# A fused attention and mixer kernel: words of U, V and the first weights moved to other steps, the first low-rank rows split by VectorE, V's second copy made by one transfer, the first product's beginning reordered

## The chip, the cores and the metric

The kernel runs on one core of one Trainium2 chip. The metric is the device time of one execution in microseconds (us). Before the change three runs gave 650.47, 652.05 and 653.36 us, a median of 652.05 us. A core has a TensorE for matrix products (PE in the profile; its weight loads are PEld), a VectorE (DVE), a ScalarE (ACT), a GpSimd (POOL), and a SyncE (SP) that here only issues DMA transfers. Each engine works through its own list of instructions in order and waits for others by semaphores. Matrix products write PSUM; everything else lies in SBUF or in DRAM.

## The reference

The first half is attention with a decaying state. For each of 4 batches and 8 heads the sequence of 768 is cut into blocks of 64. A block's output is its masked scores times v, plus its scaled queries times a state that every block passes on:

```python
    for b in range(nb):
        intra = np.einsum('bhic,bhjc->bhij', qb, kb) * Dmask[None]
        intra = np.einsum('bhij,bhjd->bhid', intra, vb)
        inter = np.einsum('bhid,bhde->bhie', qb * lam_pow[None], kv_state)
        out[:, :, sl] = intra + inter
        kv_state = lam_block[None, :, None, None] * kv_state + np.einsum('bhsd,bhse->bhde', kb_dec, vb)
```

The heads are put side by side to x of shape (4, 768, 512). The second half mixes x along the sequence through a product of rank 32 and adds a two-layer network:

```python
    xt = x.transpose(0, 2, 1)
    h = xt @ U @ V
    u = x + h.transpose(0, 2, 1)
    ch = np.maximum(u @ w_ch1, 0.0) @ w_ch2
    return (u + ch).astype(np.float32)
```

U is 768x32, V 32x768, w_ch1 512x2048, w_ch2 2048x512. These four arrive as float64 and are turned into float32 on the chip: the kernel reads them as pairs of 32-bit words.

## The kernel before

**Steps of the front.** The attention half is a list of 24 steps, one for each tile of 128 rows of the sequence: steps 0 to 5 are batch 0, 6 to 11 batch 1, and so on. The list `pieces` is written out by hand, and every engine gets its instructions in that order; no scheduler changes it. A step s holds, among others: the transposes of the next tile's q and k on TensorE (L361) and their copies by ScalarE (qt, kt, L367), the products of weights with v (px, L459), the state's product (pkv, L431) and its sum by VectorE (kv, L437, L439, L442), the products with the state (L470), the copy of the result to x by ScalarE (x_nat, L476), the next scores (pss, L408) and their masking by VectorE (sm, L417). GpSimd scales q (qs, L392) and k (ks, L381). Each step loads 256 KB each of q, k and v some steps ahead (L282): q and k are issued by SP, v by ScalarE's queue.

**The mixer inside the front.** At the end of a batch (s = 5, 11, 17) `low` multiplies the batch's x by U (pp, L486) and ScalarE copies that to p_f (L495). `low_rows` then makes two steps: `own`, which cuts each of four groups of 32 rows into a high part (ScalarE, L532) and a low part (GpSimd, L533) within the tile `vp`, and `other`, four transfers on SP that copy them to the neighbouring group (L543). From step 7 on `mix` (L566) multiplies V's rows by them, and x is corrected (L578), transposed (L629), split (L643, L644, L636) and stored (L594). TensorE reaches the first `mix` after step 7's products.

**Words turned to weights, aside.** U, V and the first two column blocks of w_ch1 are converted in small pieces that hang on steps: `side` maps a step's number to pieces, and `aside(s)` issues them at a place of step s. Each conversion has the pieces: the load of words (SP, L146), *one* (VectorE, L166 and L155, and two ScalarE activations, L173 and L174), *two* (L184), *three* (L192), *four* (L197). What a piece gives to ScalarE is put off to the place `late` of the same or the next step. V then is cut: VectorE makes the high part (`five`, L719), ScalarE copies it to two groups of rows of `vp` (four copies, L726), and VectorE and GpSimd make the low part for one group each (L730). A column block of w_ch1 has three more: *five* (ScalarE, L215), *six* (VectorE, L220), *seven* (VectorE, L227).

**The first product.** After step 23 the PSUM pools change and `hidden` runs units: two groups of 512 rows (a pair) against one block of w_ch1, 16 products to pz (L838), 8 to pd (L849), then ScalarE and VectorE join them (L845, L854) and SP stores r. The first units use the four groups that are ready; in between, as the list `rest` says by unit and place, the last batch is finished: its `low` (L486), its rows, the products pu (L573) and their sums (x_nat, L574), the transposes `turn` (put, L607) with their split (L612, L613, L616). The last pieces of the second block of w_ch1 follow units 0 and 1. There are 48 units in all, then 96 steps of the second product (L970, L972, L974); from unit 4 on the change touches nothing.

Of the kernel before, what the change touches and what calls it, by code (L numbers as in the profile page):

```python
# [8 lines left out]
FP32 = mybir.dt.float32  # L9
F32R = mybir.dt.float32r  # L10
U32 = mybir.dt.uint32
# [7 lines left out]
def kernel(  # L19
# [84 lines left out]
    def tmp(name):  # L104
        return wconv.tile([P, C], FP32, tag="tmp", bufs=2, name=name)
# [391 lines left out]
    def low_rows(b):  # L497

        pp = pps.pop(b)
        own = [(slice(g * R, (g + 1) * R), slice(g * P, (g + 1) * P)) for g in range(G)]  # L500
        if b == B - 1:
            t = tmp("p_h")[0:R]
            h, h2, l, l2 = (p_hl[g * R : (g + 1) * R] for g in range(G))
            for rows, cols in own:
                nc.vector.tensor_scalar(
                    t[:, cols].bitcast(U32), pp[rows].bitcast(U32), HI, None, ALU.bitwise_and
                )

            def low_part():
                for rows, cols in own:  # L510
                    nc.vector.tensor_tensor(
                        out=l[:, cols], in0=pp[rows], in1=t[:, cols], op=ALU.subtract
                    )

            def spread():
                nc.scalar.copy(h, t)
                nc.scalar.copy(h2, t)

            def spread_low():
                nc.scalar.copy(l2, l.bitcast(FP32))  # L520

            pps[b] = [spread, low_part, spread_low]
            return


        def place(g, of, low):
            return p_hl[g * R : (g + 1) * R, low * 2 * P + (of % 2) * P :][:, 0:P]

        def own():
            for g in range(G):  # L530
                rows, at = pp[g * R : (g + 1) * R], place(g, g, 0)
                nc.scalar.copy(at, rows)  # L532
                nc.gpsimd.tensor_tensor(  # L533
                    out=place(g, g, 1), in0=rows, in1=at.bitcast(FP32), op=ALU.subtract
                )

        def other():
            for g in range(G):
                at, of = (
                    p_hl[x * R : (x + 1) * R].rearrange("r (l h c) -> r l h c", l=2, h=2)  # L540
                    for x in (g ^ 1, g)
                )
                nc.sync.dma_start(  # L543
                    out=at[:, :, g % 2].bitcast(FP32), in_=of[:, :, g % 2].bitcast(FP32)
                )

        pps[b] = [own, other]
# [105 lines left out]
    for s in range(NS):  # L653
# [8 lines left out]
        step += [("split", done - 1)] * turns  # L662
        step += [("next_of_low", b - 1)] * (s == NT)
        step += [("prep", s + 1)] * more
# [16 lines left out]
        step += [("masked", s + 1)] * more  # L681
        step += [("low_rows", b)] * (more and c == NT - 1)
        step += [("aside", s)] * (s in (0, NT - 2, NT - 1, NT))
        step += [("store", done)] * (done >= 0 and done // TG < FG)
# [17 lines left out]
    def v_steps():  # L702
# [7 lines left out]

        def parts(gs):
            for half in range(2):
                rows, cols = slice(half * R, (half + 1) * R), slice(half * SH, (half + 1) * SH)
                for g in gs:
                    yield v_hl[g * R : (g + 1) * R, cols], rows

# [7 lines left out]
        def high():  # L724
            for out, rows in parts((0, 2)):
                nc.scalar.copy(out, st["t"][rows])  # L726

        def low(g, engine):
            for out, rows in parts((g,)):
                engine.tensor_tensor(  # L730
                    out=out, in0=st["v"][rows], in1=st["t"][rows], op=ALU.subtract
                )

        halves = [moe_V[:, half * SH : (half + 1) * SH] for half in range(2)]
        return weight_steps(dst, halves, SH, 2 * R, in_parts=True) + [
            five, lambda: low(1, nc.vector), lambda: low(3, nc.gpsimd),
        ]

# [5 lines left out]
    for steps, at in (  # L744
        (u_side, (-1, 1, 1, 2, 2)),
        (v_steps(), (0, 0, 3, 3, 4, 4, 4, 5, 5)),
        (w1_steps(0, True, True), (8, 9, 10, 11, 12, 14, 15, 16, 17, 17, 20, 21)),
        (w1_steps(1, True, True), (14, 15, 16, 17, 18, 22, 23, NS, NS, NS, NS, NS)),
    ):
        assert len(steps) == len(at)  # L750
        for step, n in zip(steps, at):
            side.setdefault(n, []).append(step)
# [24 lines left out]
    for name in "vkvq":  # L777
        load_next(name)
    aside(-1)
    load_next("k")  # L780
# [13 lines left out]
    on_scalar_late(NS)  # L794
    last = side.pop(NS)
    assert not side
    front_ctx.close()
# [87 lines left out]
    def run_units(units, side, every=lambda i: None):  # L885
# [11 lines left out]
        (0, 14, "next_of_low", b), (0, 14, "next_of_low", b), (0, 14, "next_of_low", b),  # L897
        (0, 18, "turn", c0 - 1), (0, 22, "mix", c0),
    ]
# [7 lines left out]
    head = [(pair, ft) for two in (pairs[:2], pairs[2:]) for ft in (0, 1) for pair in two]  # L907
    side = list(zip((0, 0, 0, 0, 1), last)) + list(zip((0, 3, 3, 3, 4, 4, 4, 4), w1_steps(2)))
    for i, (pair, ft) in enumerate(head):
# [164 lines left out]
```

## Time and profile before

| what | value |
|---|---|
| runs shown | 650.47, 652.05, 653.36 us; median 652.05 us |
| the profiled execution's own time | 651.64 us |
| its span, first to last instruction | 649.8 us |
| PE busy | 639.3 us (98% of the span) |
| DVE, ACT, POOL busy | 435.9, 268.1, 116.6 us |
| granted TensorE clock | 1.000 |
| transfers | 131.69 MB, mean 203 GB/s |
| span of the front (steps 0 to 23) | 0 to 114.8 us |
| units 0 and 1 of the first product | 114.8 to 131.6 us |

The profile is of one execution. Its times start at the first instruction. A view of waits puts the idle time of an engine down to what ended it; "issue" is time in which an engine waited for nothing that the profile shows. A timeline's line gives start, duration, engine, line of the kernel, operation and tiles. A view by windows gives the busy time of each engine in a stretch and, at its end, the granted clock, the mean share of the 16 DMA engines and the GB/s that they moved; that share adds up the times of packets and passes 1 where they overlap.

### The profile page before, as it was taken

The page shows a single profiled execution, that of the slowest core. Times are in us where ns is not written, and L with a number is a line of the kernel's source. Part 1 is how long each engine was busy: PE and PEld are TensorE (multiplying, and loading weights), DVE is VectorE, ACT ScalarE, POOL GpSimd, SP SyncE. Part 2 cuts the span into 40 slices and gives each one's busy share as a digit, 9 for nine tenths or more (in the row PEclk, how much of TensorE's full clock was granted, in tenths as well). Part 3 has the DMA queues.
Part 4 walks back from the last instruction along what each step waited for, and adds up shares of the span by engine and source line. Part 5 has one row for each costly group of instructions (what it writes and reads, how often), then busy time and mean ns, then how long its engine had stood idle before and what let it go on. Part 6 is the DMA issues. An engine that isn't in the chain of part 4 may idle for free.

```text
span 649.8 us, 13407 instructions
## 1 busy us (share of the span) xinstructions
PE 639.3 (98%) x5242; PEld 538.5 (83%) x5242; DVE 435.9 (67%) x713; ACT 268.1 (41%) x497; POOL 116.6 (18%) x104
## 2 busy tenths in 40 slices
PE   9999989999999999999999999999999999999997
PEld 8889989788888888888888888888888888888886
DVE  6666868668997777777796244675575665755854
ACT  4675756435664444444455221332322322322320
POOL 4475968240000000000000000030030300300300
PEclk9999999999999999999999999999999999999999
DMA  9989985264776655565587999864363363453521
GB/s 227 249 208 250 249 218 159 84 209 169 287 274 210 211 210 211 210 211 211 210 291 261 325 333 381 301 209 149 97 226 98 114 210 98 161 163 98 178 82 65
DMA packets 132737, 131.69 MB, mean 203 GB/s; under 512 B 81538, under 2 KB 90754, under 8 KB 132674
## 3 DMA queue, kind: packets, MB, share of 16 engines
q1 hardware_dynamic: 107552, 124.41, 58.9%
q10 hardware_dynamic: 25122, 6.42, 4.4%
q8 instruction: 41, 0.67, 0.4%
q14 instruction: 22, 0.18, 0.1%
HBM read 80.09 MB, written 50.33 MB: 201 GB/s over the span
## 4 chain that ended last, share of the span: by engine, by line
PE 94%; ACT 2%; DMA 1%; DVE 1%; issue 1%; ACTq 0%; DVEq 0%
PE pz L838 26%; PE pz L972 13%; PE pz L970 13%; PE pd L974 13%; PE pd L849 13%; PE px L459 4%; PE pss L408 3%; PE px L470 2%; PE pqk L361 2%; PE pkv L431 1%; PE pm L566 1%; DMA qraw<-in_q_dram 1%; PE pp L486 1%; DMA kraw<-in_k_dram 1%; PE pm L629 1%
## 5 line engine op out<-in xcount | busy, mean ns | idle before, releaser
L838 PE MATMUL pz<-u_hl,w 128*128 128x512 f32 x768 | 184.4, 390 | 0.0
L838 PEld LDWEIGHTS pz<-u_hl,w 128*128 128x128 f32 x768 | 143.6, 188 | 30.1 <-ACT r L845 0.3
L972 PE MATMUL pz<-w_hl,m 128*128 128x512 f32 x384 | 148.6, 389 | 0.0
L970 PE MATMUL pz<-w_hl,m 128*128 128x512 f32 x384 | 148.3, 389 | 0.0
L974 PE MATMUL pd<-w_d,m 128*128 128x512 f32 x384 | 147.3, 389 | 0.0
L953 ACT ACTIVATE m<-rm 128x512 fp32r<-128x512 f32 x96 | 60.6, 632 | 182.4 <-PE pd L974 130.4
L954 DVE SCALAR_TENSOR_TENSOR m<-rm,m 128x512 fp32r<-128x512 f32 x96 | 71.5, 747 | 95.8 <-ACT m L953 95.8
L999 POOL TENSOR_TENSOR o<-o,u 128x512 f32<-128x512 f32 x20 | 29.8, 1521 | 433.0 <-DVE o L995 433.0
L854 DVE SCALAR_TENSOR_TENSOR r<-pd,r 128x512 f32<-128x512 f32 x96 | 61.7, 684 | 60.5 <-ACT r L845 48.2
L849 PE MATMUL pd<-u_d,w 128*128 128x512 f32 x384 | 95.9, 390 | 0.0
L970 PEld LDWEIGHTS pz<-w_hl,m 128*128 128x128 f32 x384 | 72.1, 188 | 15.1
L972 PEld LDWEIGHTS pz<-w_hl,m 128*128 128x128 f32 x384 | 72.1, 188 | 14.9
L974 PEld LDWEIGHTS pd<-w_d,m 128*128 128x128 f32 x384 | 72.1, 188 | 14.9
L849 PEld LDWEIGHTS pd<-u_d,w 128*128 128x128 f32 x384 | 71.8, 188 | 14.8
L845 ACT ACTIVATE r<-pz 128x512 f32<-128x512 f32 x96 | 51.7, 590 | 65.0 <-PE pz L838 65.0
L955 DVE SCALAR_TENSOR_TENSOR m<-m 128x512 fp32r<-128x512 f32 x96 | 74.7, 779 | 3.0
L417 DVE TENSOR_TENSOR sm<-pss,mask 128x512 f32<-128x512 f32 x48 | 30.9, 684 | 18.6 <-PE pss L408 18.6
L215 ACT ACTIVATE w<-wf 128x512 fp32r<-128x512 f32 x32 | 20.3, 633 | 38.6 <-DVE wf L197 30.7
L173 ACT ACTIVATE sc<-sc,ends 128x512 f32<-128x512 uint32 x30 | 21.6, 720 | 22.8 <-DVE sc L166 22.8
L459 PE MATMUL px<-vraw,sm 128*64 128x64 f32 x768 | 28.3, 225 | 1.0 <-issue 0.7
L408 PE MATMUL pss<-qt,kt 64*128 64x128 f32 x384 | 28.6, 289 | 0.4 <-ACT kt L367 0.4
L392 POOL TENSOR_TENSOR qs<-qt,powq 128x512 f32<-128x512 f32 x20 | 26.0, 1300 | 15.3 <-ACT qt L367 15.1
(92 smaller groups left out, 606.5 us busy)
## 6 DMA issues: line engine op xcount, KB each, us to landing
r_d<-r SPq DMA_DIRECT2D x96, 256.0 KB, 2.5
rm<-r_d SPq DMA_DIRECT2D x96, 256.0 KB, 2.7
words<-in_moe_w_ch_dram SPq DMA_DIRECT2D x30, 512.0 KB, 4.3
w_d<-w SPq DMA_DIRECT2D x16, 768.0 KB, 3.4
w_hl<-w_d SPq DMA_DIRECT2D x16, 512.0 KB, 6.0
u_d<-x_nat SPq DMA_DIRECT2D x24, 256.0 KB, 4.1
u<-u_d SPq DMA_DIRECT2D x24, 256.0 KB, 4.3
qraw<-in_q_dram SPq DMA_DIRECT2D x23, 256.0 KB, 4.8
```

The lines of the kernel that those rows point to most:

```text
L408: nc.tensor.matmul(out=pss[:, x, a, :], lhsT=kt[half[x], a, :], rhs=qt[half[x], a, :], start=True, stop=True,)
L459: nc.tensor.matmul(out=px[half[t], x, a, :], lhsT=sm[:, x, a, half[t]], rhs=vr[:, 2 * a + x, :], start=(a == 0), stop=(alone and a == HP - 1),
L838: nc.tensor.matmul(out=like(acc[g][0], g), lhsT=w[:, n, ct, :], rhs=columns(uhl[g][:, n], g, ct), start=(ct == 0 and n == 0), stop=(ct == ...
L845: nc.scalar.mul(rs[g], acc[g][0], 4096.0 + 1.0)
L849: nc.tensor.matmul(out=like(acc[g][1], g), lhsT=w[:, 2, ct, :], rhs=columns(ud[g], g, ct), start=(ct == 0), stop=(ct == CT - 1),)
L854: nc.vector.scalar_tensor_tensor(rs[g], acc[g][1], 4096.0, rs[g], ALU.mult, ALU.add)
L953: nc.scalar.activation(out=m[:, 0], in_=r, func=AF.Relu, scale=NEAR)
L954: nc.vector.scalar_tensor_tensor(m[:, 1], r, 0.0, hi, ALU.max, ALU.subtract)
L955: nc.vector.scalar_tensor_tensor(m[:, 2], hi, E, low, ALU.mult, ALU.subtract)
L970: nc.tensor.matmul(out=pz, lhsT=m[:, 0, cols], rhs=hl[:, 0], start=first, stop=False)
L972: nc.tensor.matmul(out=pz, lhsT=m[:, 1, cols], rhs=hl[:, 1], start=False, stop=end)
L974: nc.tensor.matmul(out=pd, lhsT=m[:, 2, cols], rhs=dd, start=first, stop=end)
```

## The change

1. U's words are loaded in step 1 and not ahead of step 0; *one* and *two* run in step 3, *three* and *four* in step 4.
2. V's words are loaded in step 2; *one* and *two* in step 4, *three*, *four*, `five` and `low` in step 5. ScalarE copies the high part to one group (two copies), VectorE makes one low part, and one SP transfer (`again`, 64 partitions of 768 elements) copies both to the other two groups; GpSimd has no part in it.
3. The first batch's `own` runs in step 5. VectorE cuts off the high part from p_f (one 128x128 instruction) and copies it to the four groups; GpSimd's four subtractions read it. ScalarE does none of it. For batches 1 and 2 `own` is as before.
4. The words of w_ch1's block 0 are loaded in steps 6, 7, 9, 11 (before 8 to 11), those of block 1 in steps 18 to 21 (before 14 to 17), its *one* in step 22 (before 18).
5. *three* to *six* of block 1 run ahead of the first product's unit 0, not behind it; *seven* behind unit 0, not unit 1.
6. The last batch's rows: ScalarE copies the four high parts straight from PSUM, VectorE subtracts, ScalarE makes the second copies. The second `turn` of unit 0 stands at place 15, not 18.

On the engines' lists the order of TensorE's instructions changes in that one `turn` alone. VectorE's list of step 5 and 6 reads: sm of step 6, the cut of p_f, four copies, V's *three*, *four*, `five`, two of `low`, kv of step 7, sm of step 7.

```diff
         def own():
+            high = tmp("p_h")[:, 0:P] if b == 0 else None
+            if b == 0:
+                nc.vector.tensor_scalar(
+                    high.bitcast(U32), pp.bitcast(U32), HI, None, ALU.bitwise_and
+                )
             for g in range(G):
                 rows, at = pp[g * R : (g + 1) * R], place(g, g, 0)
-                nc.scalar.copy(at, rows)
-                nc.gpsimd.tensor_tensor(
-                    out=place(g, g, 1), in0=rows, in1=at.bitcast(FP32), op=ALU.subtract
-                )
+                if b == 0:
+                    nc.vector.tensor_copy(out=at, in_=high[g * R : (g + 1) * R])
+                    top = high[g * R : (g + 1) * R]
+                else:
+                    nc.scalar.copy(at, rows)
+                    top = at.bitcast(FP32)
+                nc.gpsimd.tensor_tensor(out=place(g, g, 1), in0=rows, in1=top, op=ALU.subtract)
...
-        step += [("next_of_low", b - 1)] * (s == NT)
...
+        step += [("next_of_low", b)] * (s == NT - 1)
...
         def high():
-            for out, rows in parts((0, 2)):
+            for out, rows in parts(0):
                 nc.scalar.copy(out, st["t"][rows])
-        def low(g, engine):
-            for out, rows in parts((g,)):
-                engine.tensor_tensor(
+        def low():
+            for out, rows in parts(1):
+                nc.vector.tensor_tensor(
                     out=out, in0=st["v"][rows], in1=st["t"][rows], op=ALU.subtract
                 )
+            on_scalar(again)
+
+        def again():
+            nc.sync.dma_start(out=v_hl[half[1]].bitcast(FP32), in_=v_hl[half[0]].bitcast(FP32))
...
-        (u_side, (-1, 1, 1, 2, 2)),
-        (v_steps(), (0, 0, 3, 3, 4, 4, 4, 5, 5)),
-        (w1_steps(0, True, True), (8, 9, 10, 11, 12, 14, 15, 16, 17, 17, 20, 21)),
-        (w1_steps(1, True, True), (14, 15, 16, 17, 18, 22, 23, NS, NS, NS, NS, NS)),
+        (u_side, (1, 3, 3, 4, 4)),
+        (v_steps(), (2, 2, 4, 4, 5, 5, 5, 5)),
+        (w1_steps(0, True, True), (6, 7, 9, 11, 12, 14, 15, 16, 17, 17, 20, 21)),
+        (w1_steps(1, True, True), (18, 19, 20, 21, 22, 22, 23, NS, NS, NS, NS, NS)),
...
-    aside(-1)
...
+    for step in last[:4]:
+        step()
...
-        (0, 18, "turn", c0 - 1), (0, 22, "mix", c0),
+        (0, 15, "turn", c0 - 1), (0, 22, "mix", c0),
...
-    side = list(zip((0, 0, 0, 0, 1), last)) + list(zip((0, 3, 3, 3, 4, 4, 4, 4), w1_steps(2)))
+    side = list(zip((0,), last[4:])) + list(zip((0, 3, 3, 3, 4, 4, 4, 4), w1_steps(2)))
```

And the last batch's rows:

```diff
-            t = tmp("p_h")[0:R]
             for rows, cols in own:
-                nc.vector.tensor_scalar(
-                    t[:, cols].bitcast(U32), pp[rows].bitcast(U32), HI, None, ALU.bitwise_and
-                )
+                nc.scalar.copy(h[:, cols], pp[rows])
             def low_part():
                 for rows, cols in own:
                     nc.vector.tensor_tensor(
-                        out=l[:, cols], in0=pp[rows], in1=t[:, cols], op=ALU.subtract
+                        out=l[:, cols], in0=pp[rows], in1=h[:, cols].bitcast(FP32),
+                        op=ALU.subtract,
                     )
             def spread():
-                nc.scalar.copy(h, t)
-                nc.scalar.copy(h2, t)
+                nc.scalar.copy(h2, h.bitcast(FP32))
...
-            pps[b] = [spread, low_part, spread_low]
+            pps[b] = [low_part, spread, spread_low]
```

More of the change, by code (lines that the diff above doesn't have):

```diff
@@ L709, in dst, with parts @@
             return st["v"]
-        def parts(gs):
+        def parts(g):
             for half in range(2):
                 rows, cols = slice(half * R, (half + 1) * R), slice(half * SH, (half + 1) * SH)
-                for g in gs:
-                    yield v_hl[g * R : (g + 1) * R, cols], rows
+                yield v_hl[g * R : (g + 1) * R, cols], rows
         def five():
@@ L724, in high @@
         def high():
-            for out, rows in parts((0, 2)):
+            for out, rows in parts(0):
                 nc.scalar.copy(out, st["t"][rows])
-        def low(g, engine):
-            for out, rows in parts((g,)):
-                engine.tensor_tensor(
+        def low():
+            for out, rows in parts(1):
+                nc.vector.tensor_tensor(
                     out=out, in0=st["v"][rows], in1=st["t"][rows], op=ALU.subtract
                 )
-        halves = [moe_V[:, half * SH : (half + 1) * SH] for half in range(2)]
+            on_scalar(again)
+        def again():
+            nc.sync.dma_start(out=v_hl[half[1]].bitcast(FP32), in_=v_hl[half[0]].bitcast(FP32))
+        halves = [moe_V[:, i * SH : (i + 1) * SH] for i in range(2)]
         return weight_steps(dst, halves, SH, 2 * R, in_parts=True) + [
-            five, lambda: low(1, nc.vector), lambda: low(3, nc.gpsimd),
+            five, low,
         ]
```

## Prediction
> **What bounds the kernel now.** I read the page first: engines, slices, then the chain of waits. TensorE is busy 98% of the span and carries 94% of the chain, so a wait is worth something only where TensorE stops for it.
>
> ```profile
> PE 639.3 (98%) x5242; PEld 538.5 (83%) x5242; DVE 435.9 (67%) x713; ACT 268.1 (41%) x497; POOL 116.6 (18%) x104
> PE 94%; ACT 2%; DMA 1%; DVE 1%; issue 1%; ACTq 0%; DVEq 0%
> DMA  9989985264776655565587999864363363453521
> ```
>
> The reader sees that there is little to win, and that the transfers run full in the first six slices (to 97 us), which is the front. Next the chain by time, from 0 to 46 us:
>
> ```profile
> 10.59 5.89 DMA qraw<-in_q_dram
> ...
> 31.40 0.59 ACT x_nat L476
> 31.98 0.40 ACT vp L726
> ...
> 35.56 0.58 ACT qt L367
> 36.14 0.50 ACT kt L367
> 36.64 0.04 issue
> 36.68 1.16 PE pss L408 x16
> ```
>
> TensorE waits at 16.6 us for the fourth q, and at 36.7 us for kt, behind ScalarE's eight copies of V and of the first rows. The waits of TensorE:
>
> ```profile
> PE px L470 <- issue: 1.5, 2, 0.8
> PE put L607 <- DVE x_nat L574: 1.3, 2, 0.9
> PE pqk L361 <- DMA qraw<-in_q_dram: 0.8, 2, 0.6
> PE pss L408 <- ACT kt L367: 0.4, 1, 0.4
> ```
>
> The windows from scores to scores, steps 16 and 17 against their twins 22 and 23 of the next batch (PE, PEld, DVE, ACT, POOL, clock, DMA share, GB/s):
>
> ```profile
> 77.50:82.80 5.30, 4.54 (x124) 4.21 (x124) 4.52 (x7) 2.99 (x8) 4.32 (x4) 1.00 1.09 278
> 82.80:87.60 4.80, 4.07 (x112) 3.73 (x110) 3.58 (x5) 2.21 (x4) 4.00 (x4) 1.00 1.13 283
> ...
> 106.60:111.00 4.40, 4.40 (x130) 4.16 (x126) 4.34 (x7) 3.17 (x8) 3.96 (x4) 1.00 0.18 63
> 111.00:114.80 3.80, 3.74 (x97) 3.43 (x97) 2.79 (x6) 1.18 (x2) 1.96 (x2) 1.00 0.21 75
> ```
>
> The same steps take 5.3 and 4.8 us at a DMA share of 1.1, and 4.4 and 3.8 us at 0.2; the two "issue" waits on px lie in the two long ones. Last, VectorE against GpSimd in the timeline:
>
> ```profile
> 22.65 0.34 DVE L166 TENSOR_SCALAR sc<-words 64x384 uint32<-64x384 uint32 x1
> 22.82 1.31 POOL L392 TENSOR_TENSOR qs<-qt,powq 128x512 f32<-128x512 f32 x1 [2.45 <-ACT qt L367]
> 22.91 1.42 DVE L155 TENSOR_SCALAR m<-words 64x384 uint32<-64x384 uint32 x1
> 24.37 0.55 DVE L184 SCALAR_TENSOR_TENSOR m<-words,m 64x384 f32<-64x384 uint32 x1
> ```
>
> Two equal VectorE instructions take 0.34 and 1.42 us. The second began inside GpSimd's qs and ended 0.2 us behind it (24.13): it waited out a whole GpSimd instruction. sm (L417), with one input in PSUM, is 0.68 us whatever GpSimd does.
>
> **The change part by part**, on the profiled execution (651.64 us, 0.41 under the median).
>
> *U's and V's words later.* SP issues U for 1.76 us at 8.06 and only then k and the q that is late (issued 10.59, landed 16.47). Without U's 192 KB, at that window's 258 to 283 GB/s, it lands some 0.7 us sooner, which is the wait of 0.64. I take -0.64 (bounds -0.8, with the 0.19 at 11.99, and 0). SP passes U and V behind more q and k; those are needed later than they land. VectorE's pieces of U leave steps 1 and 2, where TensorE did not wait for them; in step 4 U's *three*, *four* and V's *one*, *two* (rows of 0.36 to 0.67 us) fit between sm at 29.9 and 32.5.
>
> *V and the first rows in steps 5 and 6.* ScalarE loses four copies of 0.31 (L532) and two of 0.52 (L726) ahead of qt: the 0.42 of kt goes, so scores 7 start at about 35.6, not 36.68. What is late next is VectorE. Before, its list between sm of step 6 and sm of step 7 had 1.11 (L730) and kv, and sm of step 7 began as its scores ended. Now it has, from p_f on (33.57 with the -0.64): the cut (0.21, from the 0.25 of a 128x192 tensor_scalar), four copies (no row; 0.16 is the 64x4 copy, 0.3 the same rows from PSUM; I take 0.24), *three* 0.41, *four* 0.55, `five` 0.35, `low` 1.11: 3.6 us. Free of GpSimd that ends at 37.2, and px of step 7, half of sm later, starts at 38.25 instead of 38.69. But GpSimd has just then four subtractions (0.45 each), qs 1.28 and ks 1.06, ready one behind the other. If each VectorE instruction of that list waits for the GpSimd instruction in front, as L155 above, the copies lose 1.0, *three* 0.35, *four* 1.2 (qs) and `five` 1.0 (ks), 3.5 in all: px of step 7 starts at 41.7, 3.0 us later than before, with the two gains already in it. If GpSimd always went first, copies included, it would be 42.5. So between -0.4 and +3.8 I take +3.0, being nearest to the rows of L155 and of L192 (1.22 us for 128x192 beside ks).
>
> [...]
>
> *One transfer for V's second copy.* `again` waits for the last `low` (40.6) on SP; behind it stand words, k and q for three steps ahead, which have slack. The 32 KB copies landed in 1.8 to 3.5 us, U's 192 KB in 5.7. At 3 us it lands at 43.6; `mix` is wanted at 44.0 (px 41.7, then 1.24, 0.47 and 0.62). I take 0; the upper bound is 46.3, +2.3.
>
> *First-layer words.* The 128 KB loads leave steps 14 to 17, a tenth of what those steps move, and 8 and 10. Against their twins steps 16 and 17 lose 1.0 and 1.0 us, and step 9 loses 0.48 (4.79 from scores to scores, 4.31 in step 15). All of it would be -2.5; if the full queue still stops TensorE, 0; in steps 18 to 20 (share 1.13 at 97.9 to 102.3) the loads may make one such stop, +0.5. I take -1.6: the share falls to about 1, neither row's. Block 1's *one* now stands in step 22 behind kv and beside GpSimd's u_d, ahead of the last sm, for which TensorE waits: +0.3 (0 to 0.4, the 0.42 of the instruction).
>
> *The product's beginning.* put waits for x_nat, 0.40 at 125.18 and 0.87 at 129.69. The first x_nat stood behind a split that waited for a `turn` now earlier; the second behind *three*, *four*, *six* (0.68, 0.69, 0.69) and a ScalarE copy, now done by 118.7. Both go: -1.27. ScalarE's put split slips 0.9 behind *five*; its rows still are ready at 121.6, as TensorE comes to them at 122.3. Bounds -1.5 (with the 0.26 on r) and +0.5.
>
> Sum: +3.0 - 1.6 + 0.3 - 1.3 = +0.4: 652.0 for an execution like the profiled one, 652.4 as median.
>
> **The rivals.**
>
> *VectorE gets through.* If its next instruction takes the turn before GpSimd (L166 and L155 at 14.14 to 15.02 ran as a pair while ks started), px of step 7 starts at 38.3: 652.4 - 3.4 = 649.0, and 648.1 with all of the words' gain. Against it: the chain *three* to `low` is dependent, with a gap at each link.
>
> *TensorE falls to half pace.* The list above leaves it without work from 37.2 to 41.7. At the start the chain has the first scores at 1.97 us for 16 (1.09 later), the transposes at 0.85 (0.49), the state at 0.99 (0.61): 1.6 us lost before it was at pace. If a gap of 4.5 us brings that back: 654.0, slower, and 655.6 if a wait in front of `mix` brings it back twice; it decides from the point where the gap is long enough, which no row before tells, since TensorE never stopped over 1 us. [...]
>
> *The one transfer is late.* At U's 5.7 us: 652.4 + 2.3 = 654.7, with a wait of TensorE in front of `mix` in step 7.
>
> *The words do not matter.* The stops come again in steps 16 and 17: +1.6 (or 2.1 with one more later), 654.0 to 654.5.
>
> **How the numbers follow.** Half a per cent, 3.3 us, is about what a measurement of this kernel tells from no change. The likeliest has 0.35 (652.4, its own range 650.5 to 654, all within). VectorE gets through: 0.28, of which 0.21 below 648.8, as its two times lie on both sides. Half pace 0.2, of which 0.13 above 655.3 (once or twice); late transfer 0.1, half of it above, with the 0.8 us of GpSimd going first on top; no gain from the words 0.07, of which 0.03 above in the same way. So faster 0.21, same 0.58, slower 0.21. The range leaves out a tenth on either side: 648.0 to 656.0.
>
> **What would show it.** At 33 to 42 us: VectorE instructions of V at over 1 us beside qs and ks, kv and sm of step 7 late, TensorE idle ahead of px until about 41.7 and no wait for kt. In 73 to 92 us a DMA share near 1 and steps of 4.3 us. No wait of put for x_nat at 125 to 131. Wrong would make it: sm of step 7 beginning below 39, a wait of TensorE for `again` or for words in step 22, or first scores' pace (1.97 us for 16) behind step 7.

## The result, and the profile after

The changed kernel takes 653.93 us (median of 15 runs, 652.05 to 657.49), the kernel before 651.06 us beside it (15 runs, 649.54 to 654.77). The ratio is 1.0032, with a 95% interval of 1.0017 to 1.0046: slower by about 2.1 us (1.1 to 3.0), within the half per cent that was called no change. The ratio on record is not that of the two medians, which lie 2.9 us apart; differences in us behind a ratio are worked out from the ratio. Of all runs of this study one counts as disturbed, a run of e1 with 716.1 us, and that kernel's ratio leaves it out. The profiled execution has a span of 651.4 us, 1.6 more than the one before.

The page of the changed kernel: the engines, the chain of waits by engine, the granted TensorE clock and the share of the DMA engines by slices.

```profile
PE 639.9 (98%) x5242; PEld 539.8 (83%) x5242; DVE 438.2 (67%) x714; ACT 266.5 (41%) x494; POOL 114.8 (18%) x102
PE 95%; ACT 1%; DMA 1%; DVE 1%; issue 1%; POOL 0%; ACTq 0%; DVEq 0%; SPq 0%; POOLq 0%
PEclk9989999999999999999999999999999999999999
DMA  9969897264776655565577999865363363443521
```

Little has moved in the sums. What is new is one slice, the third, in which the granted clock is not full (32 to 49 us). The waits of TensorE in the changed kernel (total, times, longest):

```profile
PE px L459 <- ACT kt L367: 4.1, 1, 4.1
...
PE pqk L361 <- DMA kraw<-in_k_dram: 0.6, 1, 0.6
PE pm L571 <- DMA vp<-vp: 0.5, 1, 0.5
PE px L459 <- ACT u_hl L648: 0.4, 1, 0.4
```

One wait of 4.1 us stands where none stood before. The waits of put for x_nat and the one for kt ahead of step 7's scores are gone; 0.5 in front of `mix` (in step 13) and 0.4 in step 22 are new. So is the 0.6 for the second k, at 5.4 us, but before the change the first of the loads that it moves went out only at 8.06 us. The chain of waits from 33 to 42 us shows what the 4.1 us are made of (start, duration, what):

```profile
33.55 0.27 ACT p_f L495
...
33.85 0.24 DVE p_h L529
...
34.11 0.21 DVE vp L535
...
34.36 0.37 DVE vp L535
...
34.76 0.49 DVE vp L535
...
35.28 0.50 DVE vp L535
...
35.81 0.83 DVE sc L192
...
36.66 1.52 DVE vf L197
...
38.20 1.11 DVE vt L723
...
41.72 1.69 PE px L459 x32
```

From p_f on the chain runs on VectorE: the cut of the first rows, four copies, then V's *three*, *four* and `five` at 0.83, 1.52 and 1.11 us. From `five` on the profile's chain goes over ScalarE (V's high part, qt, kt), and it puts the wait of px down to kt. But px starts 0.79 us behind the start of sm (40.93), as in the kernel before (0.80), where kt ended only behind the start of px. So px waits for sm, which stands on VectorE's list behind `five`, `low` and kv. GpSimd's rows in the timeline of the same stretch tell why the pieces are so long:

```profile
34.16 2.06 POOL L540 TENSOR_TENSOR vp<-p_f,p_h 32x128 fp32r<-32x128 f32 x4 [3.29 <-DVE p_h L529]
36.29 1.47 POOL L392 TENSOR_TENSOR qs<-qt,powq 128x512 f32<-128x512 f32 x1
37.72 1.37 POOL L381 TENSOR_TENSOR ks<-kraw,small 128x512 f32<-128x512 f32 x1
```

*three* ends (36.63) behind the last subtraction (36.22), *four* (38.17) behind qs (37.76), `five` (39.30) behind ks (39.09). px of step 7 starts at 41.72, and its 32 products take 1.69 us, where the same group takes 1.10 to 1.29 in the other steps from step 1 on. The windows of the 4.1 us, of px, of the state's product and of the products with the state show why (columns as in the prediction's windows: the clock is the third number from the end):

```profile
37.67:41.72 4.05, 0.00 (x0) 0.03 (x1) 3.91 (x7) 1.98 (x4) 2.22 (x3) 1.00 0.31 73
41.72:43.41 1.69, 1.69 (x37) 1.69 (x39) 0.50 (x1) 0.00 (x0) 0.47 (x1) 0.61 0.94 214
43.41:44.27 0.86, 0.86 (x21) 0.74 (x21) 0.00 (x0) 0.00 (x0) 0.00 (x0) 0.50 1.08 246
44.27:45.33 1.06, 1.06 (x34) 0.94 (x34) 0.86 (x4) 0.00 (x0) 0.98 (x1) 0.50 0.92 212
```

The granted clock is 0.61, 0.50 and 0.50 behind the gap: this is half pace, and the trace dates it from 42.11 to 45.52 us. The scores of step 8 start at 45.71, against 41.28 before: +4.43.

The windows from scores to scores that answer to those of before, steps 16 and 17 (columns as there):

```profile
81.99:86.31 4.32, 4.32 (x126) 4.08 (x125) 3.62 (x7) 3.17 (x8) 3.12 (x4) 1.00 1.14 281
86.31:90.09 3.78, 3.78 (x110) 3.58 (x109) 3.03 (x6) 2.21 (x4) 3.78 (x4) 1.00 1.18 274
```

The two steps take 4.3 and 3.8 us, 1.0 less each than before, and the two "issue" waits are gone. But the DMA share is 1.14 and 1.18, higher than the 1.09 and 1.13 of before, although the words' loads have left these steps.

Start by start, the profiled execution is 0.67 us ahead at the scores of step 7, 4.43 behind at step 8, 4.51 at step 16 (0.48 won in step 9, 0.74 lost in step 13), 2.50 at step 18, 2.89 at the first product. From the first to the 65th product of pz it takes 29.13 us and not 30.54. 2.89 less 1.41 is 1.5, nearly all of the 1.6.

### The profile page after: what moved, and what is told of

It reads as the page before. It is cut to its first block, busy times and chain, and to the rows that moved or that the text cites. A ratio compares the mean times of both kernels' runs of the same rounds, so it can differ in the third digit from the quotient of the medians.

```text
span 651.4 us, 13398 instructions
## 1 busy us (share of the span) xinstructions
PE 639.9 (98%) x5242; PEld 539.8 (83%) x5242; DVE 438.2 (67%) x714; ACT 266.5 (41%) x494; POOL 114.8 (18%) x102
## 4 chain that ended last, share of the span: by engine, by line
PE 95%; ACT 1%; DMA 1%; DVE 1%; issue 1%; POOL 0%; ACTq 0%; DVEq 0%; SPq 0%; POOLq 0%
PE pz L847 27%; PE pd L858 13%; PE pz L981 13%; PE pz L979 13%; PE pd L983 13%; PE pss L408 4%; PE px L459 3%; PE px L470 2%; PE pqk L361 2%; PE pkv L431 1%; PE pm L571 1%; PE pp L486 1%; DMA kraw<-in_k_dram 1%; PE put L612 1%; PE pm L634 1%
## 5 line engine op out<-in xcount | busy, mean ns | idle before, releaser
L417 DVE TENSOR_TENSOR sm<-pss,mask 128x512 f32<-128x512 f32 x48 | 30.9, 684 | 18.9 <-PE pss L408 18.9
L215 ACT ACTIVATE w<-wf 128x512 fp32r<-128x512 f32 x32 | 20.3, 633 | 36.5 <-DVE wf L197 28.7
L459 PEld LDWEIGHTS px<-vraw,sm 128*64 128x64 f32 x768 | 26.1, 142 | 6.5 <-ACT kt L367 4.2
```

The source lines that it names most:

```text
L417: nc.vector.tensor_tensor(out=sm[:, x], in0=pss[:, x], in1=mask[:, x], op=ALU.mult)
L459: nc.tensor.matmul(out=px[half[t], x, a, :], lhsT=sm[:, x, a, half[t]], rhs=vr[:, 2 * a + x, :], start=(a == 0), stop=(alone and a == HP - 1),
```

## The experiments

**The parts one by one.** Four kernels were run beside the kernel before (median 652.36 of 35 runs).

The parts on U, V and the first rows alone (e1):

```diff
-        (u_side, (-1, 1, 1, 2, 2)),
-        (v_steps(), (0, 0, 3, 3, 4, 4, 4, 5, 5)),
+        (u_side, (1, 3, 3, 4, 4)),
+        (v_steps(), (2, 2, 4, 4, 5, 5, 5, 5)),
...
+                    nc.vector.tensor_copy(out=at, in_=high[g * R : (g + 1) * R])
```

> Only U's and V's words later, the first rows by VectorE and V's second copy by one transfer; words of w_ch1 and the product's beginning as before. Theory (VectorE's list, drawn out by GpSimd, holds up step 7, and TensorE starts again at half pace): px of step 7 starts at 41.5 to 42, its 32 products take about 1.7 us and not 1.25, scores of step 8 come 4.4 us later than before, and nothing later gives it back: ratio 1.0067 (1.005 to 1.008), +4.4 us. The stops of px in steps 16 and 17 and the two waits of put on x_nat stay. Rival (the loss is made up later, because what stops TensorE afterwards are transfers, which then have 4 us more): +2 us or less, ratio below 1.003.

Measured: 656.51 us, ratio 1.005 (1.003 to 1.007), about +3.3 us. Its products at step 7 in the timeline (start, duration; in brackets the idle time before):

```profile
43.33 1.88 PE L459 MATMUL px<-vraw,sm 128*64 128x64 f32 x32 [4.46 <-ACT kt L367]
44.94 1.13 PE L431 MATMUL pkv<-vraw,ks 128*64 128x64 f32 x16
45.99 1.08 PE L470 MATMUL px<-kv,qs 64*64 64x64 f32 x32
```

The gap and the slow products behind it are there without the rest of the change. This profile had lost 2.1 us in two "issue" stops by then (20.3 and 30.9 us), which is why px starts at 43.3; the gap itself is what the theory said. Nothing later gave it back.

The words of w_ch1 alone (e2):

```diff
-        (w1_steps(0, True, True), (8, 9, 10, 11, 12, 14, 15, 16, 17, 17, 20, 21)),
-        (w1_steps(1, True, True), (14, 15, 16, 17, 18, 22, 23, NS, NS, NS, NS, NS)),
+        (w1_steps(0, True, True), (6, 7, 9, 11, 12, 14, 15, 16, 17, 17, 20, 21)),
+        (w1_steps(1, True, True), (18, 19, 20, 21, 22, 22, 23, NS, NS, NS, NS, NS)),
```

> Only the words of w_ch1 in other steps. Theory (loads out of the full stretch end the two stops of px): steps 16 and 17 lose 1 us each, step 9 0.5, step 22 gains 0.3: -2.2 us, ratio 0.9966 (0.996 to 0.998). Rival (the gain in the profile of the whole change came because the front ran 4 us later against its transfers, not by the words): the two stops stay, ratio 0.999 to 1.001.

Measured: 652.41 us, ratio 1.0004 (0.9978 to 1.0029). The gain of 2.2 us is not there. The stops of steps 16 and 17 are gone in this profile too, but it has a longer one elsewhere, in step 3, before any of these words are loaded:

```profile
21.79 0.49 PE L408 MATMUL pss<-qt,kt 64*128 64x128 f32 x4 [2.14 <-issue]
```

The product's beginning alone (e3):

```diff
-            pps[b] = [spread, low_part, spread_low]
+            pps[b] = [low_part, spread, spread_low]
...
+    for step in last[:4]:
+        step()
...
-        (0, 18, "turn", c0 - 1), (0, 22, "mix", c0),
+        (0, 15, "turn", c0 - 1), (0, 22, "mix", c0),
```

> Only the last rows by ScalarE, the weight pieces ahead of unit 0 and the earlier turn. Theory: both waits of put on x_nat go, 0.40 and 0.87: -1.3 us, ratio 0.998 (0.997 to 0.999); the front is unchanged to within 0.3 us. Rival (ScalarE's put split, now behind its piece of the weights, holds up unit 1): no gain, ratio 0.9995 or above.

Measured: 651.39 us, ratio 0.9983 (0.9957 to 1.0009), about -1.1 us, with an interval that includes no change. In the profile TensorE waits for x_nat no more, and from the first to the 65th product of pz it takes 29.14 us, as in the whole change, and not 30.54.

Words and beginning, without the parts on U, V and the first rows (e4, shown against the whole change):

```diff
-        (u_side, (1, 3, 3, 4, 4)),
-        (v_steps(), (2, 2, 4, 4, 5, 5, 5, 5)),
+        (u_side, (-1, 1, 1, 2, 2)),
+        (v_steps(), (0, 0, 3, 3, 4, 4, 4, 5, 5)),
```

> The whole change without the parts on U, V and the first rows. Theory: the two gains add, -2.2 and -1.3, -3.5 us, ratio 0.9946 (0.9935 to 0.9965), faster than both kernels; the whole change is this plus about 4.4 and the 0.7 of step 13. Rival (the gains hang on the front running later): -1.3 us, ratio 0.998, and the difference to the whole change is then not the 5 us that the theory gives but 3.4.

Measured: 650.76 us, ratio 0.998 (0.9956 to 1.0003), about -1.3 us: what the beginning is worth alone, and 2.2 less than was expected. By ratios the parts give +3.3, +0.3 and -1.1, together +2.5, and the whole change +2.1. They add up with a word term of nothing, as far as this can tell: the interval of each part is 1.3 to 1.7 us to either side.

**What draws out VectorE's list.** In the whole change, two GpSimd instructions were left out, the scaling of q for step 7 and of k for step 8 (e5):

```diff
-        if s % NT > 0:
+        if s == NT + 1:
+            st[s]["qs"] = st[s]["qt"]
+        elif s % NT > 0:
             st[s]["qs"] = qs = att.tile([P, HP, P], FP32, tag="qs", bufs=2, name="qs")
...
-        if s % NT < NT - 1:
+        if s == NT + 2:
+            st[s]["ks"] = raw[s, "k"].rearrange("p (a x) d -> p a x d", x=2)
+        elif s % NT < NT - 1:
```

> The whole change, but GpSimd leaves out the scaling of q in step 7 and of k in step 8 (the unscaled tiles are used, so the outputs of batch 1 are other numbers). Theory (V's pieces on VectorE wait out these two GpSimd instructions): three, four and five, 0.82, 1.51 and 1.10 us with them, take about 0.41, 0.55 and 0.35; px of step 7 starts at about 39.5 and not 41.7; TensorE's idle time ahead of it is 1.9 and not 4.05 us; scores of step 8 come 2.2 us earlier than in the change, and 2.6 if the shorter gap also leaves TensorE at pace: ratio 0.9995 (0.998 to 1.001). Rival (the list itself is too long, whatever GpSimd does): the three pieces stay over 0.8 us and px starts later than 41.

Measured: 651.21 us beside 651.79 of before (29 runs), ratio 0.9995 (0.9976 to 1.0014). VectorE and TensorE in its timeline:

```profile
35.01 0.82 DVE L192 SCALAR_TENSOR_TENSOR sc<-words,sc 64x384 uint32<-64x384 uint32 x1
35.86 0.55 DVE L197 SCALAR_TENSOR_TENSOR vf<-m,sc 64x384 f32<-64x384 f32 x1
36.45 0.35 DVE L727 TENSOR_SCALAR vt<-vf 64x384 uint32<-64x384 uint32 x1
...
39.22 1.24 PE L463 MATMUL px<-vraw,sm 128*64 128x64 f32 x32 [2.66 <-ACT kt L367]
40.29 0.64 PE L435 MATMUL pkv<-vraw,ks 128*64 128x64 f32 x16
40.85 0.69 PE L474 MATMUL px<-kv,qt 64*64 64x64 f32 x32
```

*four* and `five` fall from 1.52 and 1.10 to 0.55 and 0.35 us: the waiting behind qs and ks is shown. *three* stays at 0.82: the four subtractions were left in, and it ends 0.41 us behind the last of them (35.83 and 35.42), as in the changed kernel (36.63 and 36.22); that was missed in the expectation. With a gap of 2.66 us the three groups behind it take 1.24, 0.64 and 0.69 in this execution, as in a step without a gap. Its mean granted clock is 0.999, but ten of this kernel's 12 runs have 0.996 or 0.997, so this one execution does not speak for all.

**What pushes V under GpSimd.** The whole change, with the first batch's rows as before (e6):

```diff
         def own():
-            high = tmp("p_h")[:, 0:P] if b == 0 else None
...
-                if b == 0:
-                    nc.vector.tensor_copy(out=at, in_=high[g * R : (g + 1) * R])
-                    top = high[g * R : (g + 1) * R]
-                else:
-                    nc.scalar.copy(at, rows)
-                    top = at.bitcast(FP32)
+                nc.scalar.copy(at, rows)
...
-        step += [("next_of_low", b)] * (s == NT - 1)
+        step += [("next_of_low", b - 1)] * (s == NT)
```

> The whole change, but the first batch's rows are cut by ScalarE and GpSimd in step 6 as before; V's pieces stay in step 5. Theory (it is the five instructions on the first rows, from 33.8 to 35.8, that push V's pieces under GpSimd's qs and ks): three begins at about 33.7, low ends before 37.5, px of step 7 starts at 38.5 to 39, scores of step 8 near 41.3: ratio 0.998 (0.9965 to 0.9995), 3.3 us better than the whole change. Rival (V's pieces alone are too late in step 5): px of step 7 starts at 40 or later and TensorE stands over 2 us, ratio 1.000 or above.

Measured: 650.33 us beside 651.79, ratio 0.9969 (0.9948 to 0.9991): about 2.0 us faster than before, and the lowest ratio of this study (e4's 0.998 and e10's 0.9982 lie within its interval). Its timeline:

```profile
32.90 0.55 DVE L197 SCALAR_TENSOR_TENSOR vf<-m,sc 64x384 f32<-64x384 f32 x1
...
34.02 1.42 DVE L726 TENSOR_TENSOR vp<-vf,vt 32x384 fp32r<-32x384 f32 x2
...
36.49 1.29 DVE L417 TENSOR_TENSOR sm<-pss,mask 128x512 f32<-128x512 f32 x2 [0.60 <-PE pss L408]
```

V's pieces come through before qs starts at 35.83, sm of step 7 begins as its scores end, and VectorE even stands idle for 0.6 us before it. px starts at 37.29, and scores of step 8 at 40.66. So neither V in step 5 nor the list's length as such is the trouble, but the cut and the four copies in front, 1.9 us at the wrong place. What shows up instead is the one transfer: it lands at 40.35, `mix` wanted it at 39.9, and TensorE stands still for 0.51 us there, until 40.44. The profile names nothing that ended this wait; the times fit the transfer, while the last of the four transfers of the first rows had landed at 38.94. In the changed kernel the delay of step 7 hid that.

**Whether the gap costs pace.** Products of ident by ident fill it, 30 in one kernel (e7) and 15 in a second (e11):

```diff
+        if s == NT + 1:
+            idle = two_banks("idle", "px")[:, 0, 0:P]
+            for i in range(30):
+                nc.tensor.matmul(out=idle, lhsT=ident, rhs=ident, start=True, stop=True)
         st[s]["px"] = both = two_banks("px", "px")
```

> The whole change, with 30 products of ident by ident on TensorE between the transposes of step 8 and px of step 7, into the bank that px then writes anew; their result is not read. Theory (the 4 us gap drops TensorE to half pace): px of step 7 still starts at about 41.7, but its 32 products take about 1.2 us and not 1.69, the state's 16 0.65 and not 1.08, the products with the state 0.69 and not 1.13; scores of step 8 come 1.2 us earlier than in the change, unless the wait on vp takes a part of it back: ratio 1.001 (1.000 to 1.003). Rival (those durations come from waits on VectorE's two halves of sm, not from the gap): they stay at 1.7, 1.1 and 1.1.

Measured: 657.4 us (6 runs), ratio 1.0082 (1.0056 to 1.0109). The 30 products take 6.96 us, so px had to wait for them and started at 43.62; that is where the time went. The paces behind it were 1.15, 0.64 and 0.69. With 15 of them:

> The whole change with 15 products of ident by ident in the gap ahead of px of step 7, half as many as before, at 0.23 us each 3.5 us, so that px need not wait for them. Theory (the gap drops TensorE to half pace): px, the state and the products with the state take 1.24, 0.65 and 0.70 us; scores of step 8 come 1.2 us earlier than in the change: ratio 1.0015 (1.000 to 1.003). Rival (half pace costs nothing further on, since a wait on vp or on transfers takes it back): as the change, ratio 1.003.

Measured: 653.35 us beside 652.15 (35 runs), ratio 1.0009 (0.9985 to 1.0032). The timeline of TensorE (it lists each of the 15 products as two):

```profile
37.02 3.62 PE L456 MATMUL idle<-ident 128*128 128x128 f32 x30
41.56 1.24 PE L463 MATMUL px<-vraw,sm 128*64 128x64 f32 x32 [0.92 <-PE idle L456]
42.62 0.64 PE L431 MATMUL pkv<-vraw,ks 128*64 128x64 f32 x16
43.19 0.69 PE L474 MATMUL px<-kv,qs 64*64 64x64 f32 x32
43.81 0.50 PE L575 MATMUL pm<-vp 64*128 64x256 f32 x4
44.15 1.05 PE L408 MATMUL pss<-qt,kt 64*128 64x128 f32 x16
```

From px to the scores of step 8 it is 2.59 us, as in the kernel before (38.69 to 41.28), and in the change 3.99. The gap of 4 us thus costs 1.4 us more than its own length, and useless products in it give that back. By ratio 1.5 us came back; its interval alone would not carry that, the timeline does. The mean granted clock of each run agrees: it is 0.997 or less in all 15 runs of the changed kernel and in all 12 of e1, and in one of 12 with the 15 products.

**Two attempts at a better version.** U and V in steps 1 to 5 on another plan, V by the one transfer, the new beginning, all the rest as before (e8):

```diff
-        (u_side, (-1, 1, 1, 2, 2)),
-        (v_steps(), (0, 0, 3, 3, 4, 4, 4, 5, 5)),
+        (u_side, (1, 2, 2, 3, 3)),
+        (v_steps(), (2, 2, 3, 3, 4, 4, 4, 5)),
```

> The kernel before with the reordered beginning of the product, U's and V's words loaded in steps 1 and 2, V's pieces in steps 3 and 4 (low in step 5) with the one transfer for the second copy; the first rows by ScalarE and GpSimd, and the words of w_ch1, as before. Theory: the waits at 16.6 (0.6), for kt in step 7 (0.4) and both of put (1.3) go, and nothing is pushed under GpSimd in step 5: px of step 7 near 38.2, ratio 0.9965 (0.995 to 0.998), faster than both kernels. Rival (V's pieces in steps 3 and 4 hold up sm there, since U's pieces now stand in steps 2 and 3): a new wait of TensorE before 30 us, ratio 0.998 to 1.000.

Measured: 653.56 us beside 651.79, ratio 1.0024 (1.0004 to 1.0045). The rival came: TensorE waits 2.4 us for sm of step 3.

```profile
21.07 0.26 DVE L166 TENSOR_SCALAR sc<-words 128x192 uint32<-128x192 uint32 x1 [3.00 <-DMA words<-in_moe_U_dram]
...
21.53 1.38 DVE L184 SCALAR_TENSOR_TENSOR m<-words,m 128x192 f32<-128x192 uint32 x1
22.84 1.27 DVE L417 TENSOR_TENSOR sm<-pss,mask 128x512 f32<-128x512 f32 x2
```

U's *one*, ahead of sm on VectorE's list, waits for words that were loaded only one step earlier, and *two* then takes 1.38 us beside a qs (21.43 to 22.69) and ends 0.22 us behind it. The second attempt is e6, with V's high part copied by VectorE and the transfer on ScalarE's queue (e10):

```diff
-            on_scalar(high)
-        def high():
             for out, rows in parts(0):
-                nc.scalar.copy(out, st["t"][rows])
+                nc.vector.tensor_copy(out=out, in_=st["t"][rows])
...
-            nc.sync.dma_start(out=v_hl[half[1]].bitcast(FP32), in_=v_hl[half[0]].bitcast(FP32))
+            nc.scalar.dma_start(out=v_hl[half[1]].bitcast(FP32), in_=v_hl[half[0]].bitcast(FP32))
```

> The whole change with the first rows as before (as in the run that was best so far), and with V's high part copied by VectorE and the one transfer issued by ScalarE's queue, ahead of step 8's qt. Theory: the transfer is issued near 36.2 and not at 37.5, lands before the products of V's rows want it at 39.5, and the wait of 0.5 there goes; qt of step 8 comes 0.5 earlier: ratio 0.996 (0.9945 to 0.9975). Rival (two more VectorE instructions beside GpSimd's four subtractions make sm of step 7 late): px of step 7 starts later than 38 and the gain is lost, ratio 0.997 or above.

Measured: 651.32 us beside 652.15, ratio 0.9982 (0.9959 to 1.0005). The rival again:

```profile
34.37 1.02 DVE L719 CAST vp<-vt 32x384 fp32r<-32x384 f32 x2
35.41 2.27 DVE L723 TENSOR_TENSOR vp<-vf,vt 32x384 fp32r<-32x384 f32 x2
35.79 1.46 POOL L392 TENSOR_TENSOR qs<-qt,powq 128x512 f32<-128x512 f32 x1
```

1.02 us more on VectorE's list, and the two subtractions run into qs: 2.27 us and not 1.42. px starts at 38.95. The wait of 0.5 in front of `mix` in step 7 is gone, but with px this late that shows nothing of the other queue.

**Whose the stops are.** The words were loaded twice in the kernel before (e9), and the kernel before was run once more unchanged (e12):

```diff
+    spares = iter(range(8))
...
                 nc.sync.dma_start(out=out, in_=in_)
+                if in_parts and len(loads) == 4:
+                    spare_d = dram.tile([P, 2 * P], U32, name=f"spare_d{next(spares)}")
+                    nc.sync.dma_start(out=spare_d, in_=in_)
```

> The kernel before, with each of the eight loads of w_ch1's words in the front followed by a second one of the same 128 KB into a spare place in DRAM. Theory (the words' bytes in the full stretch stop TensorE): the stops in steps 8 to 11 and 14 to 17 grow as they were expected to shrink, +1.2 to +2.5 us, ratio 1.002 to 1.004. Rival (the stops come at fixed places of TensorE's list, one in about 126 products, and which of them is long changes from execution to execution; the words decide nothing): below 1.001, and the profile has stops at other members of that row.

> The kernel before, not changed at all. Theory (the stops of px in steps 16 and 17 are the words'): both are there again with 0.6 to 0.9 us. Rival (fixed places, changing lengths): stops of 0.2 to 2 us at other members of the row of places, and steps 16 and 17 of about 4.3 and 3.8 us in spite of the words. Ratio 1.000 (0.998 to 1.002) by both.

Measured: 655.04 us with the words twice, ratio 1.0031 (1.0008 to 1.0054), and 651.76 unchanged, ratio 0.9985 (0.996 to 1.0011). The windows of the unchanged kernel, steps 16 and 17:

```profile
77.22:81.54 4.32, 4.32 (x126) 4.08 (x125) 3.89 (x7) 3.18 (x8) 3.39 (x4) 1.00 1.16 295
81.54:85.50 3.96, 3.96 (x110) 3.71 (x109) 3.21 (x6) 2.21 (x4) 3.96 (x4) 1.00 1.09 283
```

With all words where they were and a share of 1.16 and 1.09, the steps take 4.3 and 4.0 us. The stops of 0.75 us that the forecast was made from belong to one execution, not to the kernel. Counting TensorE's products from the first, the stops (over 0.12 us) that fall on a row of places 125 to 127 products apart, or a multiple of that, are these, in the front of each profile:

```
words as before   product number (us)
  before          1101 (0.27), 1986 (0.75), 2113 (0.73)
  e12             1227 (0.17), 2240 (0.56)
  e1              344 (0.83), 595 (1.27), 1481 (0.54), 2240 (0.84), 2618 (0.58)
  e3              595 (0.17)
  e8              2240 (0.42)
words moved
  after           722 (0.19)
  e2              344 (2.14), 470 (0.63), 595 (0.14), 723 (0.26), 1481 (0.51)
  e4              344 (0.69), 595 (0.17), 1101 (0.82)
  e5              1986 (0.28), 2113 (0.45), 2240 (0.55)
  e6              none
  e7              2240 (0.32)
  e10             722 (0.49), 2113 (0.68)
  e11             595 (0.72)
words twice
  e9              344 (2.34), 723 (0.52), 1354 (0.21), 2113 (0.18), 2240 (0.83)
```

The places are the same in all, also in e7 and e11, where the useless products count with the rest; which of them is long, and whether any is, differs from execution to execution, from nothing to 4.1 us in sum. With the words as before the mean is 1.4 us, with the words moved 1.1: a difference far within the spread. The rival of both expectations stands for the stops.

What stands ahead of a stop's end is in the traces too. The page counts 41 packets, 0.67 MB in all, on a DMA queue that it calls instruction (shown below), and the trace has the times of each. One comes ahead of each place of the row; at four of the stops:

```
profile, product   packet moved      stop            TensorE goes on behind the packet
before, 1986       79.83 to 80.80    81.45 to 82.20  1.40
before, 2113       84.91 to 85.87    86.59 to 87.32  1.45
e2, 344            19.12 to 20.38    19.65 to 21.79  1.41
e9, 344            19.78 to 20.71    19.70 to 22.04  1.33
```

In all 33 stops of the list TensorE goes on 1.24 to 1.57 us behind the end of that place's packet, whatever the length of the stop. In the other profiles the packet of product 344 set out between 15.67 and 17.96 us, in e2 and e9 at 19.12 and 19.78. So the end of each stop follows a packet of this queue; that TensorE waited for instructions in that packet is inferred from these times. What set the packets' times is not shown.

For the bytes it does not stand wholly. Loading the words twice did cost: the interval of its ratio leaves out no change. In its profile 2.34 us are a stop in step 3, ahead of the first of these loads, and half pace follows (the granted clock is 0.50 from 23.0 to 26.4 us):

```profile
22.04 0.49 PE L412 MATMUL pss<-qt,kt 64*128 64x128 f32 x4 [2.34 <-issue]
...
23.86 1.92 PE L463 MATMUL px<-vraw,sm 128*64 128x64 f32 x32
```

What can be the loads' doing is elsewhere than expected, in step 13, where the second batch's rows come late over SP's queue:

```profile
73.84 0.35 PE L570 MATMUL pm<-vp 64*128 64x256 f32 x1 [1.04 <-DMA vp<-vp]
74.90 0.47 PE L570 MATMUL pm<-vp 64*128 64x256 f32 x3 [0.71 <-DMA vp<-vp]
```

One profile does not settle that. The same wait is 0.5 us in the changed kernel, 0.2 to 1.1 in seven of the others (e3 and e8, with the words as before, among them), 0.15 in e10 and absent in before, its repetition, e1 and e5; what sets it stays open.

## Why the prediction was right, and where it was wrong

The time, 653.93 us, lies in the range, and no change beyond half a per cent was called likeliest. The sum behind it has one term that was right almost to the digit, one that missed a second effect, and one that was wrong. The last two both made the forecast too low, so they did not cancel; with both put right the sum is +3.4 us (below), past the 3.3 us that were taken as the limit of no change. That the call held at +2.1 is partly luck.

- *V and the first rows, +3.0: right.* px of step 7 was put at 41.7 and started at 41.72, by the alternation that was described: copies, *three*, *four* and `five` each behind a GpSimd instruction. The experiment without qs and ks shows the mechanism, and the one with the rows as before shows which edit brings it about. The trace shows it for the plain copies too: the first of four equal copies, begun (34.11) just ahead of GpSimd's first subtraction (34.16), took 0.21 us; the other three took 0.37, 0.49 and 0.50, and each ended 0.09 us behind one of the first three subtractions (their ends are 34.64, 35.16 and 35.69).
- *The likeliest case left out half pace: this step failed.* It was priced rightly as a rival (1.6; it measured 1.4) and given 0.2, on the ground that no row before tells from which gap on. The runs tell that the changed kernel's gap, 4.05 us in its profile, does it: the mean granted clock is 0.993 to 0.997 in all 15 of them. They give no sharp point below: 2.37 us (e8) and 2.66 us (e5) did not do it in the profiled executions, 2.34 us (e9) did. By my own sum the gap was 4.5 us, and the only rows before that show TensorE below pace are those of the kernel's start (first scores 1.97 us, 1.09 later); the 0.2 was my estimate, and with 15 runs of 15 below full clock it was far too low. With this rival in the sum the forecast is 2.0 us over the kernel before, and 2.1 came; that these are so near is luck, since the words' term stood wrongly in it.
- *First-layer words, -1.6: wrong.* The step "against their twins steps 16 and 17 lose 1.0 and 1.0 us" took one execution's stops for the kernel's; the two ended 1.40 and 1.45 us behind a packet of the instruction queue, and no run shows that the words set them. The profile of the changed kernel seems to bear the term out (-2.0 in these steps, -0.48 in step 9), and would have been taken for proof. The words alone measure +0.3 us (-1.4 to +1.9), and the unchanged kernel ran the same steps without stops. That the DMA share would fall to about 1 was wrong as well: 1.14 and 1.18.
- *Block 1's* one *in step 22, +0.3: right.* 0.38 us in front of px of step 23 in the changed kernel, 0.23 to 0.39 in the others with the words moved, and in none without. The profile puts the wait down to u_hl, but px starts 0.78 us behind sm (115.07), as in step 7, and sm stood behind *one*, whose second instruction took 1.51 us beside GpSimd's u_d.
- *U's and V's words later, -0.64, and kt, -0.42: right in kind.* No kernel with U's load moved waits at 16.6 us, against 0.6, 0.6 and 0.3 us in three with it early (before, e12, e4); but three more with it early (e2, e3, e9) did not wait either, so the wait is not the kernel's every time. The wait for kt went as the ScalarE copies went.
- *One transfer, 0: right.* It landed at 43.38 (43.6 was put down), and `mix` was reached at 45.3, behind the slow products. The term hangs on step 7 being late: where it is in time, in e6, the transfer seems to cost 0.5.
- *The product's beginning, -1.3: right.* -1.4 by the profile, -1.1 by the ratio of this part alone (its interval includes no change).
- *Not foreseen:* the 0.74 us lost in step 13.

Put together with what the runs showed: +3.0, +1.4, 0, +0.3 and -1.3 give +3.4, and the parts as run gave +2.5; the whole change gave +2.1, with 3.0 as the upper end. The rest may be the waits that the kernel before does not have every time (16.6 us, kt), which were counted as gains in full; that was not tried.

## What to carry to other kernels

A stop that the trace puts down to nothing, and that differs between two steps that should be twins, is to be looked for in a second profile of the same kernel before a gain is reckoned from it. Small VectorE work placed in front of a deadline is priced with the GpSimd instructions that become ready beside it: 1.9 us of cut and copies put step 8 back by 4.3 (45.71 against 40.66 without them, 0.73 of which was there at step 7), because it moved the pieces behind them under two GpSimd instructions (*four* and `five` took 1.52 and 1.11 us there, and 0.55 and 0.35 with the two left out) and opened a gap of 4.05 us after which TensorE ran at a granted clock of 0.50 for 3.4 us. When one term of a forecast opens a gap, the gap's own consequence (here 1.4 us) belongs in the likeliest case.

## What the runs showed of the hardware that was not expected

**Stops at fixed places of TensorE's list.** They come 125 to 127 products apart or a multiple of that, and a product as the profile counts it is two instructions, a weight load and a matmul. The page counts 5242 of each, and among the DMA queues it has one for instructions:

```profile
q8 instruction: 41, 0.67, 0.4%
```

0.67 MB in 41 packets are about 16 KB each, and 2 x 5242 instructions in 41 packets are 256 in each, or 128 products; that instructions which are not counted as busy make up the difference to 125 to 127 is an estimate. So the places would fit borders between packets of TensorE's instructions. That the queue is TensorE's is inferred from this count and from the times above: in 33 stops out of 33 TensorE goes on 1.24 to 1.57 us behind a packet's end. In this front (a DMA share of 1.09 to 1.18 in the windows of steps 16 and 17) a single stop took up to 2.34 us (e9), and their sum went from 0 (e6) to 4.1 us (e1, e9) between executions. The effect under study is 2.1 us.

**Idle time ahead of half pace.** After 4.05 and 4.46 us without work TensorE's first three groups took 1.69 to 1.88, 1.08 to 1.13 and 1.08 to 1.13 us instead of 1.24, 0.64 and 0.69. The granted clock of the whole execution shows it only as 0.996 in place of 1.000, its windows as 0.50; the 0.996 of the changed kernel also holds 1.7 us at 0.50 at the execution's end (649.7 to 651.4 us), with no product left to run. In e1 and e9, as in the changed kernel, the stretch at a half that follows the gap lasts 3.4 us. There is no fixed length of idle time in these runs from which on it happens; it is more often found behind longer gaps. Runs with a mean granted clock of 0.997 or less are none of 12 in e10 (gap of 1.65 us in the profile), 7 of 12 in e8 (2.37), 10 of 12 in e5 (2.66), and all of the changed kernel (4.05) and of e1 (4.46). It also shows in the spread of the kernel before: of its 99 runs beside the experiments 14 have such a clock, with a mean of 654.9 us, and the other 85 a mean of 652.0. Whether in these 14 a late packet of that queue came first, as in e9 (19.78 us), is not shown, since they have no profile.
